# Clustered attention and two dense layers on one core: a list scheduler gets new transfer prices, a later place for sums of squares, and 89 moved priorities

## Chip, core and metric

The kernel runs on one core of one Trainium2 chip. The metric is the device time of one execution in microseconds (us). Before the change the median of three runs is 599.44 us (597.72 to 599.91). PE is the matrix engine, PEld its weight loads, DVE the vector engine, ACT the scalar engine, POOL the third elementwise engine, and SP the engine that issues every DMA of this kernel.

## What is computed

The reference, cut to what matters (2 batches, 8 heads, 768 tokens, 64 elements a head, 16 clusters a head; 1536 tokens of 512 elements in the layers):

```python
q_assign = argmax(q_n @ c_n, -1); k_assign = argmax(k_n @ c_n, -1)   # by head
scores = where(q_assign == k_assign, (q @ k.T) / sqrt(64), -1e9)
attn = softmax(scores) ; x = attn @ v                                # 1536 x 512
h = x @ w_in ; g = h * sigmoid(1.702 * h) ; y = g @ w_out            # 512 -> 2048 -> 512
h = y @ w2_in ; solu = h * softmax(h)                                # 512 -> 1024
out = layernorm(solu) * g_ln @ w2_out                                # 1024 -> 512
```

## The kernel before

**Numbers.** Most products are made of two float16 halves, a high and a low one, in three matmuls each. To cut a weight into halves it is loaded in chunks of 128 x 512 (64-bit on the host, 512 KB a chunk), narrowed by DVE in three steps (`Weight.narrow`, lines 194, 199 and 203), squared and summed by ACT (`Weight.square`, line 216). When all chunks of a group are squared, PE adds the sums over the partitions (`bound`, `power_sum`, line 139, tile `tot`), DVE makes a power of two of them (lines 145 to 153; for `w_out` also lines 1243 to 1251), and then ACT and DVE write the high (line 237) and low (line 240) halves.

**Attention.** The 16 heads of both batches are 16 units u, two to a pair p. A pair's q and k are loaded (`load`), turned and split, their clusters found (`logits`, `cluster_...`), and the operands are put together in the tiles OP1 (64 rows of high halves, 16 of clusters, a row of maxima) and OP2 by DMAs on SP: `place_high` and `place_both` (from the tile `hl`, 64 rows of 6 KB), `place_cluster` (from `oht`, 16 rows), `peak_row` (from `mr`). There are two sets of OP tiles, and pairs take turns at them. A unit has nine steps m. `peak` (PE, line 919) makes scores whose row maxima DVE takes (line 930); `score` (PE, lines 974 and 975) makes them again with the maxima taken off; ACT takes the exponential (line 983) and the float16 high half (`cast`, line 988, sometimes DVE), POOL or DVE the low half (`rest`, line 992), and `value` (PE, lines 1007 to 1011) multiplies with v. The values' own halves are lines 777 and 784 to 790. The result of a pair is split too (`x_high`, line 1037; `x_low`, line 1041, on POOL or DVE) and transposed into `xT` by DMA (line 1047).

**First layer.** 48 blocks `Hidden` of 12 matmuls each (line 1179) follow: three of the four token blocks n, 16 column blocks m. A block is gated by ACT (line 1186), split by ACT (line 1189) and by DVE (line 1197, even m) or POOL (lines 1194 and 1195, odd m). Meanwhile `w_in`'s last three groups and all 16 chunks of `w_out` are converted.

**Order.** All of this, 1825 operations, is put in order by the class `Plan` (line 310), which is run when the program is built. Each operation has a price on each engine that can do it, a list of operations it needs, sometimes a PSUM bank that it takes or frees, and a number `due`. `Plan.order` goes through planned time: of the operations that can start first on an engine it takes the one with the lowest `due`. For SP a price is a pair, the issuing and the transfer, and transfers follow each other in one queue. What the planner finds is written out in that order, engine by engine; on the chip each engine then takes its instructions strictly one after another and waits where one is not ready. Up to 36 us of planned time, PE's planned idle time is filled with matmuls to nowhere (tile `idle`, line 1304).

**After it.** A second plan (line 1329 on, 672 operations) does the rest, from `first_project` (`w_out` on token block 0, lines 1516 to 1527) to the stores. It is the same in both kernels, and its order comes out the same.

The price of a transfer and the sum of squares before the change:

```python
T["PH", p, i] = add(dict(SP=(0.65, 1.94)), n, lambda t, i=i: place_high(p, i), ...)
a = add(
    dict(PE=0.1), NH * NU if after else d + 8, lambda t: bound(t, w.squares(c)), after=sums + (after or []),
    take="acc" if after else "ex", **kw
)
```

Of the kernel before, what the change touches and what calls it, by code (L numbers as in the profile page):

```python
# [21 lines left out]
def kernel(  # L22
# [75 lines left out]
    LN = 512.0  # L98
    WLATE = 4
    WAHEAD2 = 6  # L100
    W0, W1 = 20, 100

    const = ctx.enter_context(tc.tile_pool(name="const", bufs=1))
# [206 lines left out]
    class Plan:  # L310
# [8 lines left out]
        def __init__(self, buffers, limits, loose=False):  # L319
            self.tasks, self.buffers, self.limits, self.loose = [], buffers, limits, loose  # L320

        def add(self, cost, due, emit, after=(), take=None, frees=None, kind=None, shared=False):


            t = dict(
                cost=cost, due=due, emit=emit, after=[a for a in after if a is not None], take=take, frees=frees, kind=kind,
                shared=shared, at=None, id=len(self.tasks), users=[],
            )
            for a in t["after"]:
                a["users"].append(t)  # L330
            t["left"] = len(t["after"])
            self.tasks.append(t)
            return t

        def order(self):
# [11 lines left out]

            def possible(t, eng):
                near = self.loose and eng == "PE"
                at = max([free.get(eng, 0.0)] + [a["end" if near and a["eng"] == eng else "ready"] for a in t["after"]])  # L350
                if eng == "SP":
                    at = max(at, dma - DEPTH)
                if eng == "POOL" or (eng == "DVE" and t["shared"]):
                    at = max(at, port[0])
                if t["take"]:
                    group, limit = self.limits[t["take"]]
                    at = max(at, min(groups[group]))
                    h = sorted(x["until"] for x in held[t["take"]])
                    if len(h) >= limit:
                        at = max(at, h[len(h) - limit])  # L360
                return at
# [174 lines left out]
    def load_first(s):  # L536

        land = space(s).rearrange("p (h j d) -> p h j d", h=2, d=D)
        nc.sync.dma_start(land, (k, q)[s][0, 0:2].rearrange("h (p j) d -> p h j d", p=P))
        return land  # L540
# [120 lines left out]
    def place_high(p, i):  # L661

        move(OP1[p % NS][i][0:D], hl[p][i * D:(i + 1) * D, KH:KH + 2])

    def place_cluster(p, i, s):
        r = (2 * s + i) * C
        move(OP1[p % NS][i][D:D + C, s, :], oht[p][r:r + C, :])
# [9 lines left out]
    def late(x):  # L677

        return [T["PC", 0, 0, 1]] if x else []

    def operands_of(p):
# [3 lines left out]
        land = {}  # L685
        for s in range(2):
            if p == 0:
                a = add(dict(SP=(0.65, 1.09)), n0 - 8, lambda t, s=s: land.update({s: load_first(s)}))
                T["L", p, s, 0] = T["L", p, s, 1] = add(
                    dict(DVE=0.5), n0 - 8, lambda t, s=s: arrange(s, land[s]), after=[a], shared=True  # L690
                )
                continue
            for i in range(2):
                T["L", p, s, i] = add(
                    dict(SP=(0.65, 1.09)), n0 + LDUE if p > 1 else -62, lambda t, s=s, i=i: load(p, s, i),
                    after=[at("TT", p - 1, 2)] + late(True) if p > 1 else [],
                )
        for e in range(3):
# [40 lines left out]
        for i in range(2):  # L739
            u = 2 * (p - NS) + i  # L740
            before = [at("ST", u, NU - 1), at("SM", u, NU - 1)]
            n = n0 + 23 + 4 * i if p else n0 + 10
            T["PH", p, i] = add(
                dict(SP=(0.65, 1.94)), n, lambda t, i=i: place_high(p, i),
                after=[T["TH", p, e] for e in range(3)] + before + late(p),
            )
            for s in range(2 if p or i else 0):
                T["PC", p, i, s] = add(
                    dict(SP=(0.65, 0.14)), n - 15, lambda t, i=i, s=s: place_cluster(p, i, s),
                    after=[b] + before + ([pads[p, i]] if p < NS else []),  # L750
                )
            for e, r in enumerate((0, D)):
                T["PB", p, i, e] = add(
                    dict(SP=(0.65, 1.94)), n + 1 if p else -30 + 12 * i, lambda t, i=i, e=e, r=r: place_both(p, i, r, (QH, QL)[e]),
                    after=[T["TL", p, n] for n in range(3)] + before + late(p or i),
                )

# [39 lines left out]
    def values():  # L797

        sums = []
        for p in range(NH // 2):  # L800
            n = VDA + VDB * p if p else -50
            a = add(dict(SP=(0.47, 1.09)), n, lambda t, p=p: load_values(p), after=late(p >= VFIRST))
            sums.append(add(dict(ACT=0.82), n + 10, lambda t, p=p: values_bound(p), after=[a]))

        def powers(a, n, name):
# [55 lines left out]
    def weights(w, c, due, after=None, then=None, scores=()):  # L861


        sums, parts = [], {}
        kw = dict(tail=2 if after else 0)
        n = CV + bool(scores)
        chunks = range(c * w.group, (c + 1) * w.group)

        def step(i, k):
            if k == 0:  # L870
                parts[i] = w.narrow(i)
            next(parts[i])

        def powers(a):
            w.powers[c] = power_from(a["tile"][:, 0:w.group])
            if then:
                then()

        for i in chunks:
            d = due(i)  # L880
            prev = add(
                dict(SP=(0.47, 1.46)), d, lambda t, i=i: w.load(i),
                after=[narrows[-n] if len(narrows) >= n else None] + list(scores or late(True)), **kw
            )
            for k, x in enumerate((0.34, 0.6, 0.6) if after else (0.4, 1.0, 0.62)):
                prev = add(
                    dict(DVE=x), d + 3 + k, lambda t, i=i, k=k: step(i, k),
                    after=[prev] + (after if after and w is wo else []), shared=True, **kw
                )
            narrows.append(prev)  # L890
            sums.append(add(dict(ACT=0.61), d + 6, lambda t, i=i: w.square(i), after=[prev], **kw))
        a = add(
            dict(PE=0.1), NH * NU if after else d + 8, lambda t: bound(t, w.squares(c)), after=sums + (after or []),
            take="acc" if after else "ex", **kw
        )
        a = add(dict(DVE=0.9), NH * NU if after else d + 8, lambda t, a=a: powers(a), after=[a], frees=a, **kw)
        for i in chunks[0:WLATE if w is wo else w.group]:
            b = add(
                dict(ACT=0.61), d + 12, lambda t, i=i: w.high(i),
                after=[a, at("WL", w, i - 2)], **kw  # L900
            )
            T["WL", w, i] = add(dict(DVE=0.66 if after else 0.9), d + 13, lambda t, i=i: w.low(i), after=[b], shared=True, **kw)
# [383 lines left out]
    for p in range(NH // 2):  # L1286
# [5 lines left out]
        for u in (2 * p, 2 * p + 1):  # L1292
            scores_of(u)
    rest_of_layer()
    order = plan.order()

    idle = ps_b.tile([P, 512], F32, tag="av1", name="idle")
# [718 lines left out]
```

## Time and profile before

| | us |
|---|---|
| median of three runs | 599.44 |
| the profiled execution | 599.53 |
| its span, first to last instruction | 597.8 |
| PE busy in the span | 585.0 |
| DVE, ACT, POOL busy | 460.3, 419.2, 269.2 |
| mean granted TensorE clock | 0.997 |

The profiled execution's time is 1.7 us over its span, which is what lies around the span. The trace shows when each instruction ran, what its engine waited for before it and what ended the wait. A matmul's end is modelled, so PE's busy time hides short waits; what a stretch of PE work costs is read from where the next stretch starts.

### The profile page before, as it was taken

Reading aid. Unit: us, or ns where it says so; the run is one execution under the profiler, and the core shown is the slowest. Engines: PE = TensorE matmul, PEld = TensorE weight load, DVE = VectorE, ACT = ScalarE, POOL = GpSimd, SP = SyncE. Lnnn points to the kernel's source line nnn. Section 1 sums busy time; section 2 is a strip of 40 time slices with the busy share of each in tenths; the row PEclk is TensorE's granted clock in tenths of the full one; section 3 lists DMA queues with packets and bytes.
Section 4 is the critical chain, followed back from the end, with each engine's and each line's share of the span. In section 5 each row is a group of like instructions: output and inputs, shape, how many; then the busy total and the mean of one; then the engine's idle time right before and its main releaser. Section 6 shows DMA issues by size and latency. Waiting matters only on the chain.

```text
span 597.8 us, 12605 instructions
## 1 busy us (share of the span) xinstructions
PE 585.0 (98%) x4784; PEld 386.7 (65%) x4784; DVE 460.3 (77%) x931; ACT 419.2 (70%) x794; POOL 269.2 (45%) x255
## 2 busy tenths in 40 slices
PE   8899999999999999999989999999999999999997
PEld 6687888888888876666645666666655564444444
DVE  6989998799888989888977840884996526997820
ACT  4699989898999988778877446653656623647831
POOL 7269989666787764345653017901200300133100
PEclk9999999999999999999999999999999999999999
DMA  7997979899876127344560440230000430042561
GB/s 189 227 216 163 215 163 184 180 190 185 170 165 119 29 64 203 112 169 135 188 208 1 149 134 2 74 104 0 1 2 0 71 71 0 36 71 72 116 149 53
DMA packets 80884, 68.43 MB, mean 114 GB/s; under 512 B 63748, under 2 KB 66648, under 8 KB 80824
## 3 DMA queue, kind: packets, MB, share of 16 engines
q1 hardware_dynamic: 80824, 67.63, 47.7%
q8 instruction: 37, 0.61, 0.4%
q14 instruction: 23, 0.19, 0.1%
HBM read 34.64 MB, written 3.15 MB: 63 GB/s over the span
## 4 chain that ended last, share of the span: by engine, by line
PE 79%; DVE 11%; DMA 3%; ACT 3%; issue 2%; POOL 1%; SPq 1%; POOLq 0%; DVEq 0%; ACTq 0%
PE bank L1661 20%; PE bank L1482 16%; PE hps L1179 6%; PE bank L1179 5%; PE bank L1516 5%; PE st L974 5%; PE sm L919 5%; PE st L975 4%; PE av L1007 2%; PE av L1011 2%; PE ex L582 2%; PE av L1010 2%; DVE reg L203 2%; DVE reg L199 2%; DVE reg L194 2%
## 5 line engine op out<-in xcount | busy, mean ns | idle before, releaser
L992 POOL TENSOR_TENSOR ph<-p,ph 128x512 f16<-128x512 f32 x108 | 126.9, 1192 | 45.7 <-ACT ph L988 20.4
L1179 PEld LDWEIGHTS <-reg 128*128 128x128 f16 x768 | 75.6, 99 | 49.8 <-issue 1.7
L930 DVE TENSOR_REDUCE nma<-sm 128x1 f32<-128x512 f32 (+1 forms) x144 | 95.9, 680 | 8.8 <-PE sm L919 7.8
L1179 PE MATMUL hps<-xT,reg 128*128 128x384 f16 x576 | 96.2, 330 | 0.0
L1482 PE MATMUL bank<-g,reg 128*128 128x384 f16 x576 | 94.4, 326 | 0.0
L1482 PEld LDWEIGHTS <-reg 128*128 128x128 f16 x576 | 56.4, 98 | 37.2
L1661 PE MATMUL bank<-reg,g 128*128 128x512 f16 (+1 forms) x366 | 75.0, 365 | 0.0
L1194 POOL TENSOR_SCALAR g<-g,scl 128x384 f32<-128x384 f32 x40 | 34.2, 854 | 87.3 <-ACT g L1189 84.3
L1661 PEld LDWEIGHTS <-g 128*128 128x128 f16 x438 | 42.8, 98 | 46.8
L974 PE MATMUL st<-OP 128*128 128x256 f32 (+1 forms) x191 | 70.1, 378 | 2.3 <-DVE nma L930 1.1
L983 ACT ACTIVATE p<-st 128x512 f32<-128x512 f32 x107 | 63.6, 598 | 7.0 <-PE st L975 3.8
L975 PE MATMUL st<-OP 97*128 97x512 f32 (+3 forms) x191 | 62.8, 340 | 0.0
L1007 PE MATMUL av<-vh,ph 128*128 128x65 f16 x576 | 62.2, 194 | 0.0
L1011 PE MATMUL av<-vh,ph 128*128 128x65 f16 x576 | 61.3, 195 | 0.3 <-DVE ph L992 0.2
L1010 PE MATMUL av<-vh,ph 128*128 128x64 f16 x576 | 61.4, 193 | 0.0
L1007 PEld LDWEIGHTS <-ph 128*128 128x128 f16 x576 | 52.8, 99 | 12.5 <-issue 10.3
L919 PE MATMUL sm<-OP 80*128 80x512 f32 x192 | 57.7, 355 | 2.1 <-DMA raw<-in_moe_w_in_dram 0.7
L988 ACT CAST ph<-p 128x512 f16<-128x512 f32 x97 | 58.5, 616 | 1.2 <-PE av L1011 0.6
L1011 PEld LDWEIGHTS <-ph 128*128 128x128 f16 x576 | 53.7, 97 | 0.6 <-DVE ph L992 0.3
L1010 PEld LDWEIGHTS <-ph 128*128 128x128 f16 x576 | 53.8, 97 | 0.1
L1195 POOL TENSOR_TENSOR g<-g,g 128x384 f16<-128x384 f32 x40 | 42.1, 1052 | 3.3
L1864 POOL TENSOR_TENSOR small<-small,mhalf 128x2 f32<-128x2 f32 (+1 forms) x7 | 4.6, 656 | 80.8 <-DVE small L1860 80.8
(252 smaller groups left out, 1168.1 us busy)
## 6 DMA issues: line engine op xcount, KB each, us to landing
OP<-hl SPq DMA_DIRECT2D x48, 384.0 KB, 5.4
raw<-in_moe_w_in_dram SPq DMA_DIRECT2D x24, 512.0 KB, 4.7
raw<-in_moe_w_out_dram SPq DMA_DIRECT2D x24, 512.0 KB, 3.4
xT<-in_v_dram SPq DMA_DIRECT2D x8, 384.0 KB
raw<-in_k_dram SPq DMA_DIRECT2D x12, 192.0 KB, 6.0
raw<-in_q_dram SPq DMA_DIRECT2D x12, 192.0 KB
OP<-oht SPq DMA_DIRECT2D x30, 48.0 KB, 3.7
out_dram<-raw SPq DMA_DIRECT2D x5, 256.0 KB, 2.0
```

The source lines that it names most:

```text
L919: nc.tensor.matmul(t["tile"][:, at], Q1[0:KM, j * P:(j + 1) * P], K1[0:KM, cs], start=True, stop=True)
L930: nc.vector.tensor_reduce(out=out, in_=src, op=ALU.max, axis=AX.X, negate=True)
L974: nc.tensor.matmul(t["tile"][:, at], K2[:, ks], Q2[:, cs], start=True, stop=False)
L975: nc.tensor.matmul(t["tile"][:, at], K1[0:n, ks], Q1[0:n, cs], start=False, stop=True)
L983: nc.scalar.activation(p32s[u, m], t["tile"], AF.Exp, scale=SCALE)
L992: e.tensor_tensor(out=phs[u, m][:, 1], in0=p32s.pop((u, m)), in1=phs[u, m][:, 0], op=ALU.subtract)
L1007: nc.tensor.matmul(av[:, i, :], ph[:, 0, qs], vh[:, u, kt, D:], start=(m == 0 and i == 0), stop=False,)
L1010: nc.tensor.matmul(av[:, i, 0:D], ph[:, 0, qs], vh[:, u, kt, 0:D], start=False, stop=False)
L1011: nc.tensor.matmul(av[:, i, :], ph[:, 1, qs], vh[:, u, kt, D:], start=False, stop=(m == NU - 1 and kt == NJ - 1 and i == NJ - 1),)
L1179: nc.tensor.matmul(self.ps, w1.at(c, m, e), xT[:, x, c, n * TB:(n + 1) * TB], start=(c == 0 and e == x), stop=(c == ND - 1 and e == 1),)
L1482: nc.tensor.matmul(out_, wo.at(f, c, e), lp["g", n][:, x, f, :], start=(f == 0 and e == x), stop=(f == NF - 1 and e == 1),)
L1661: nc.tensor.matmul(out_, data, weight, start=start and i == 0, stop=stop and i == n - 1)
```

## The change

Four things are changed, all in the first plan's input. The instructions are the same but for three of the matmuls to nowhere (57 before, 54 now); only their order and, for 25 operations, the engine differ.

```diff
+    LAG = 3.0
...
-                at = max([free.get(eng, 0.0)] + [a["end" if near and a["eng"] == eng else "ready"] for a in t["after"]])
+                at = max([free.get(eng, 0.0)] + [a["end" if near and a["eng"] == eng else "ready"] + t["lag"] for a in t["after"]])
...
-                a = add(dict(SP=(0.65, 1.09)), n0 - 8, lambda t, s=s: land.update({s: load_first(s)}))
+                a = add(dict(SP=(0.65, 1.0)), n0 - 8, lambda t, s=s: land.update({s: load_first(s)}))
...
-                    dict(SP=(0.65, 1.09)), n0 + LDUE if p > 1 else -62, lambda t, s=s, i=i: load(p, s, i),
+                    dict(SP=(0.65, 1.0)), n0 + LDUE if p > 1 else -62, lambda t, s=s, i=i: load(p, s, i),
...
-                dict(SP=(0.65, 1.94)), n, lambda t, i=i: place_high(p, i),
+                dict(SP=(0.65, 2.05)), n, lambda t, i=i: place_high(p, i),
...
-                    dict(SP=(0.65, 0.14)), n - 15, lambda t, i=i, s=s: place_cluster(p, i, s),
+                    dict(SP=(0.65, 0.5)), n - 15, lambda t, i=i, s=s: place_cluster(p, i, s),
...
-            a = add(dict(SP=(0.47, 1.09)), n, lambda t, p=p: load_values(p), after=late(p >= VFIRST))
+            a = add(dict(SP=(0.47, 1.2)), n, lambda t, p=p: load_values(p), after=late(p >= VFIRST))
...
-                dict(SP=(0.47, 1.46)), d, lambda t, i=i: w.load(i),
+                dict(SP=(0.47, 1.75 if not after else 1.46)), d, lambda t, i=i: w.load(i),
...
-            take="acc" if after else "ex", **kw
+            take="acc" if after else "ex", lag=LAG, **kw
...
+    SHIFTS = {
+        57: 8, 125: -4.5, 145: 1, 163: 4.5, 182: -2, 205: 10, 206: 1.5, 241: -1.5, 250: -2.5, 255: -4, 262: -6,
...
+    }
+    for i, x in SHIFTS.items():
+        plan.tasks[i]["due"] += x
```

`place_both` gets the new price 2.05 as well. `lag` adds 3.0 us of planned time between an operation's inputs and itself; the five sums of squares of `w_in` and `w_out` have it (the later ones belong to the second plan, which has none). `SHIFTS` moves the `due` of 89 of the 1825 operations.

Three places show what comes out. The first is ACT behind the last square of `w_out` (line 216 before, 217 now; `reg_4755` and `reg_4745` are `w_out`'s tile), up to the first high half (line 237, 238). Before:

```order
L216 ACTIVATE junk,wss<-reg_4755 128x512
L1189 ACTIVATE g_4756<-hps,scl 128x384
L1186 ACTIVATE g_5628<-hps,scl 128x384
L216 ACTIVATE junk,wss<-reg_4755 128x512
L1189 ACTIVATE g_4756<-g_5628,scl 128x384
L1186 ACTIVATE hps<-hps,scl 128x384
L1189 ACTIVATE g_4756<-hps,scl 128x384
L1186 ACTIVATE g_5667<-hps,scl 128x384
L1189 ACTIVATE g_4756<-g_5667,scl 128x384
L237 ACTIVATE reg_4755<-reg_4755,scl 128x512 x2
```

Now:

```order
L217 ACTIVATE junk,wss<-reg_4745 128x512 x2
L1190 ACTIVATE g_4746<-g_5617,scl 128x384
L1187 ACTIVATE hps<-hps,scl 128x384
L1187 ACTIVATE g_5641<-hps,scl 128x384
L1190 ACTIVATE g_4746<-hps,scl 128x384
L1190 ACTIVATE g_4746<-g_5641,scl 128x384
L1187 ACTIVATE g_5661<-hps,scl 128x384
L1190 ACTIVATE g_4746<-g_5661,scl 128x384
L1187 ACTIVATE g_5681<-hps,scl 128x384
L1190 ACTIVATE g_4746<-g_5681,scl 128x384
L238 ACTIVATE reg_4745<-reg_4745,scl 128x512 x2
```

The last square is the fourth row before (five operations stand between it and the first high half) and the first row now, where two squares stand together (nine stand between). The same holds on PE: the sum `tot` of `w_out` had 48 matmuls of line 1179, four blocks, behind it and before `first_project`, and has 36 now, three blocks; one block more stands ahead of it. For `w_in`'s groups 1, 2 and 3 the sum stood behind 6, 13 and 22 blocks and stands behind 7, 16 and 23.

The second is SP's queue for pair 4 (units 8 and 9). `OP_0_0` are the tiles of unit 8, `OP_0_1` those of unit 9; 146 and 147 are OP1, 150 and 151 OP2. Before:

```order
L659 DMA OP_0_0_146<-hl 64x2x768
L659 DMA OP_0_0_150<-hl 64x2x768 x2
L659 DMA OP_0_0_146<-oht 16x768 x2
L659 DMA OP_0_1_147<-oht 16x768 x2
L659 DMA OP_0_1_147<-hl 64x2x768
L659 DMA OP_0_1_151<-hl 64x2x768
L659 DMA OP_1_1_149<-mr 1x6x128
L659 DMA OP_0_1_151<-hl 64x2x768
L530 DMA raw<-in_k_dram 128x6x64 x2
L530 DMA raw<-in_q_dram 128x6x64 x2
```

Now:

```order
L660 DMA OP_0_0_146<-hl 64x2x768
L660 DMA OP_0_0_150<-hl 64x2x768 x2
L660 DMA OP_0_0_146<-oht 16x768 x2
L184 DMA raw<-in_moe_w_in_dram 128x1024
L660 DMA OP_0_1_147<-oht 16x768 x2
L660 DMA OP_0_1_151<-hl 64x2x768
L660 DMA OP_1_1_149<-mr 1x6x128
L660 DMA OP_0_1_151<-hl 64x2x768
L531 DMA raw<-in_k_dram 128x6x64 x2
L531 DMA raw<-in_q_dram 128x6x64 x2
L660 DMA OP_0_1_147<-hl 64x2x768
```

A weight chunk has come in between the clusters of unit 8 and those of unit 9, and unit 9's `place_high` (`OP_0_1_147<-hl`) has gone from right behind the clusters to behind two `place_both`, a row of maxima and the four loads of pair 6.

The third is SP's queue for pair 6 (units 12 and 13), in the same tiles, with the transposes of an earlier pair's result (line 1047, now 1048). Before:

```order
L659 DMA OP_0_0_146<-hl 64x2x768
L659 DMA OP_1_0_148<-mr 1x6x128
L659 DMA OP_0_0_150<-hl 64x2x768 x2
L1047 DMA_TRANSPOSE xT<-xh 128x6x128 x2
L659 DMA OP_0_0_146<-oht 16x768 x2
L183 DMA raw<-in_moe_w_in_dram 128x1024
L659 DMA OP_0_1_147<-oht 16x768 x2
L659 DMA OP_0_1_147<-hl 64x2x768
L659 DMA OP_0_1_151<-hl 64x2x768
L659 DMA OP_1_1_149<-mr 1x6x128
L659 DMA OP_0_1_151<-hl 64x2x768
L183 DMA raw<-in_moe_w_in_dram 128x1024
```

Now:

```order
L660 DMA OP_0_0_146<-hl 64x2x768
L660 DMA OP_0_0_150<-hl 64x2x768
L660 DMA OP_1_0_148<-mr 1x6x128
L660 DMA OP_0_0_150<-hl 64x2x768
L1048 DMA_TRANSPOSE xT<-xh 128x6x128
L660 DMA OP_0_0_146<-oht 16x768 x2
L1048 DMA_TRANSPOSE xT<-xh 128x6x128
L660 DMA OP_0_1_147<-oht 16x768 x2
L660 DMA OP_0_1_147<-hl 64x2x768
L660 DMA OP_1_1_149<-mr 1x6x128
L660 DMA OP_0_1_151<-hl 64x2x768 x2
L184 DMA raw<-in_moe_w_in_dram 128x1024 x2
```

Unit 12's clusters (`OP_0_0_146<-oht`) stood behind both transposes and stand between them now; the weight chunk behind them has gone to the end. On DVE and POOL, three of the eight `x_low` (line 1041), those of pairs 2, 5 and 7, have moved from DVE to POOL, and one values' low half, of pair 4, from POOL (lines 784 and 785) to DVE (line 789).

## Rows read from the trace of the kernel before

**Rows 1.** Busy us by stage: length, PE, PEld, DVE, ACT, POOL, clock, DMA share, GB/s.

```profile
18.70:60.00 41.30, 38.48 (x390) 30.68 (x390) 38.97 (x88) 37.59 (x69) 27.51 (x24) 1.00 0.88 201
60.00:222.86 162.86, 160.57 (x2157) 135.97 (x2157) 146.09 (x303) 149.70 (x284) 127.12 (x106) 1.00 0.74 152
222.86:309.46 86.60, 86.60 (x547) 52.37 (x544) 78.83 (x145) 69.55 (x148) 41.63 (x40) 1.00 0.53 164
309.46:311.51 2.05, 0.01 (x2) 0.01 (x1) 1.18 (x3) 1.15 (x4) 0.30 (x1) 1.00 0.66 230
311.51:321.23 9.72, 9.72 (x51) 5.54 (x52) 6.84 (x24) 7.28 (x14) 3.00 (x4) 0.82 0.16 56
```

**Rows 2.** PE's waits, longest first: us in total, times, longest.

```profile
PE tot L139 <- ACT junk L216: 2.0, 1, 2.0
PE st L974 <- DVE nma L930: 1.1, 1, 1.1
PE st L974 <- DVE ph L992: 0.8, 2, 0.6
PE sm L919 <- DMA raw<-in_moe_w_in_dram: 0.7, 1, 0.7
PE sm L919 <- DMA OP<-oht: 0.5, 1, 0.5
```

**Rows 3.** Chain of waits, by time: start, us, what ran.

```profile
311.90 9.49 PE hps L1179 x48
321.39 31.20 PE bank L1516 x192
```

**Rows 4.** PE by time at two of its sums: start, us, instruction.

```profile
234.77 0.28 PE L139 MATMUL tot<-wss,ones 128*128 128x4 f32 x2
...
311.51 0.40 PE L139 MATMUL tot<-wss,ones 128*128 128x16 f32 x2 [2.04 <-ACT junk L216]
```

**Rows 5.** DVE by time, end of the weights' conversion.

```profile
309.97 0.67 DVE L203 SCALAR_TENSOR_TENSOR reg<-raw,reg 128x512 uint32<-128x512 uint32 x1
...
313.58 0.17 DVE L145 TENSOR_REDUCE scl<-tot 128x1 f32<-128x16 f32 x1
...
317.20 1.41 DVE L240 SCALAR_TENSOR_TENSOR reg<-reg,scl 128x512 f16<-128x512 f32 x2 [0.58 <-ACT reg L237]
```

**Rows 6.** ACT by time, the same stretch.

```profile
310.73 0.63 ACT L216 ACTIVATE junk<-reg 128x512 bf16<-128x512 f32 x1 [0.90 <-DVE reg L203]
...
311.36 0.60 ACT L1189 ACTIVATE g<-g,scl 128x384 f16<-128x384 f32 x1
...
313.52 0.61 ACT L1189 ACTIVATE g<-g,scl 128x384 f16<-128x384 f32 x1
316.44 1.33 ACT L237 ACTIVATE reg<-reg,scl 128x512 f16<-128x512 f32 x2 [2.31 <-DVE scl L1251]
```

**Rows 7.** DVE's groups from 222.8 to 311 us: busy, mean ns, idle before.

```profile
L1197 DVE SCALAR_TENSOR_TENSOR g<-hps,scl,g 128x384 f16<-128x384 f32 x21 | 12.5, 607 | 3.8 <-ACT g L1189 3.0 <-POOL g L1194 0.6
...
L1041 DVE TENSOR_TENSOR xh<-xs,xh 128x768 f16<-128x768 f32 x1 | 0.9, 947 | 0.0
```

**Rows 8.** DVE by time, first group of `w_in` that the first layer converts.

```profile
240.29 1.41 DVE L240 SCALAR_TENSOR_TENSOR reg<-reg,scl 128x512 f16<-128x512 f32 x2
```

**Rows 9.** DVE by time, a result's low half in the attention.

```profile
127.24 1.90 DVE L1041 TENSOR_TENSOR xh<-xs,xh 128x768 f16<-128x768 f32 x1
```

**Rows 10.** Groups of the whole execution, nearest prices of moved elementwise work.

```profile
L1041 POOL TENSOR_TENSOR xh<-xs,xh 128x768 f16<-128x768 f32 x5 | 8.3, 1657 | 0.9 <-ACT xh L1037 0.9
...
L1625 DVE SCALAR_TENSOR_TENSOR xT<-y,scl,xT 128x768 f16<-128x768 f32 x5 | 5.0, 1007 | 0.0
```

**Rows 11.** SP by time, loads of pair 6 and a weight chunk.

```profile
113.70 2.24 SPq L530 DMA_DIRECT2D raw<-in_k_dram  x2
...
117.47 1.25 SPq L183 DMA_DIRECT2D raw<-in_moe_w_in_dram  x1
```

**Rows 12.** PE by time, first `peak` of unit 9.

```profile
121.18 0.40 PE L919 MATMUL sm<-OP 80*128 80x512 f32 x1
```

More of the change, by code (lines that the diff above doesn't have):

```diff
@@ L320, in __init__, with add @@
             self.tasks, self.buffers, self.limits, self.loose = [], buffers, limits, loose
-        def add(self, cost, due, emit, after=(), take=None, frees=None, kind=None, shared=False):
+        def add(self, cost, due, emit, after=(), take=None, frees=None, kind=None, shared=False, lag=0.0):
             t = dict(
                 cost=cost, due=due, emit=emit, after=[a for a in after if a is not None], take=take, frees=frees, kind=kind,
-                shared=shared, at=None, id=len(self.tasks), users=[],
+                shared=shared, lag=lag, at=None, id=len(self.tasks), users=[],
             )
@@ L753, in operands_of @@
                 T["PB", p, i, e] = add(
-                    dict(SP=(0.65, 1.94)), n + 1 if p else -30 + 12 * i, lambda t, i=i, e=e, r=r: place_both(p, i, r, (QH, QL)[e]),
+                    dict(SP=(0.65, 2.05)), n + 1 if p else -30 + 12 * i, lambda t, i=i, e=e, r=r: place_both(p, i, r, (QH, QL)[e]),
                     after=[T["TL", p, n] for n in range(3)] + before + late(p or i),
```

8 rows, old and new, of the table SHIFTS are left out of this document.

## Prediction

> **What bounds the kernel now.** I read the busy time by stage first. From 222.86 to 309.46 us PE is busy for the whole stretch, and from 321.23 on the order of both kernels is the same, so what can change lies before 321.23. From 60 to 222.86 PE lacks 2.29 us, from 18.7 to 60 it lacks 2.82, and from 309.46 to 311.51 it stands still; in the stretch after that its mean granted clock is 0.82 [rows 1]. Second I read PE's waits. The longest behind the start is one of 2.0 us: `tot` waits for ACT's last square of `w_out`. The others that have a name are short and lie in the attention: for row maxima (1.1), for a low half of the exponentials (0.8), for a weight chunk ahead in a DMA queue (0.7), for the clusters `oht` (0.5) [rows 2]. Third I read the chain of waits: the first layer's last 48 matmuls take 9.49 us, while `first_project` does 192 matmuls of the same size in 31.20 [rows 3]. At that rate, 0.1625 us each, 48 take 7.80, so the four blocks behind `tot` lost 9.49 - 7.80 = 1.69 us. That is the price of the lower clock: PE came from a gap of 2.04 us [rows 4] and ran part of those blocks at the lower of its two levels, 1.2 instead of 2.4 GHz.
>
> **The last square of w_out.** DVE ends the last narrowing step at 309.97 + 0.67 = 310.64 [rows 5], ACT squares and sums at once, from 310.73, and PE, which reached the sum at 309.47, goes on at 311.51 [rows 4, 6]. Now one block more stands ahead of the sum, 12 x 0.1625 = 1.95 us, so PE reaches it at 311.42 on the old clock. DVE has a little less to do up to there: one `x_low` (0.95) and one block's low half (0.61) have gone from its order, one step of line 203 (0.67) has come in, 0.89 us less [rows 5, 7]. If DVE sets the time, the square is there at 310.6; if the chunk's DMA sets it, at 311.5. The wait is 0 to 0.1 us; I take **-2.04** for it and, since PE then comes to those blocks without a gap, **-1.69** for the clock.
>
> What becomes late next is `first_project`. Behind the sum stand 36 matmuls now, 5.85 us, so PE needs the first low half at about 311.42 + 0.24 + 5.85 = 317.5. ACT has nine operations, not five, between the last square and the first high half. Such operations came every 0.554 us (five from 311.36 to 314.13 [rows 6]), so nine take 5.0 and end at 315.6 to 316.5. DVE's powers took from 313.58 to 316.44 [rows 5, 6], 2.86 us, and cannot start before the sum; they end between 314.5 and 316.4. A high half is half of 1.33 and a low half half of 1.41 [rows 5, 6], so the first low half is there between 317.0 and 317.9. The new wait is 0 to 0.7 us; I take **+0.3**.
>
> The lag also moves the sums of `w_in`. The tight one is group 1: its sum ended at 235.05 and its last low half at 241.70, 6.65 us later [rows 4, 8]. Three blocks stand between the sum and the first matmul on that group, 5.85 us, and the fourth chunk is read by the last three of a block's twelve matmuls, 1.46 later, 7.3 in all. So it costs nothing, covered by those blocks; were the chunk needed at the block's start, it would cost 0.8, which I keep as the bound. Groups 2 and 3 have at least as many blocks as group 1.
>
> **The attention.** At pair 6 a weight chunk stood in SP's queue ahead of what unit 12's `peak` needed, and PE waited 0.7 us [rows 2]. The chunk now stands behind the operands, and unit 12's clusters stand ahead of one transpose: **-0.7** (0 to -0.7). What is late next there is nothing that the trace shows.
>
> The `x_low` of pair 2 stood on DVE ahead of a low half that PE waited for: 1.90 us from 127.24 on [rows 9], inside PE's 0.8 in two waits for `rest` [rows 2]. On POOL it costs 1.66 [rows 10] beside work of PE, but POOL makes low halves too: **-0.6** (0 to -0.8). The other two `x_low` that go to POOL end no wait.
>
> One low half of the values, pair 4, comes to DVE. No row shows line 789 on DVE at this place; the nearest of the same size is line 1625, 1.01 us [rows 10]. From 18.7 to 60 DVE is busy for 38.97 of 41.30 us [rows 1], so what is added there largely shows: **+0.5** (0 to 1.0).
>
> At pair 4 PE waits 0.5 for the clusters [rows 2], and their place behind its other operands in SP's queue is the same. In PE's new order less work stands between the turn of the clusters and that `peak`, which covers the way over DVE and SP, so the wait should grow: **+0.3** (from -0.5, the whole wait, to +0.6, half of one issue of 1.25 [rows 11]).
>
> The rest of the 89 moves and the new transfer prices reorder the same instructions. Nothing is added by them, and dense PE work up to the first products is the same. They can remove what is left of 2.29 + 2.82 us of gaps or add as much again, since DVE is busy for 94% and 90% of these two stretches [rows 1]: **0** (-2.5 to +2.5).
>
> Sum: -2.04 - 1.69 + 0.3 - 0.7 - 0.6 + 0.5 + 0.3 = **-3.9** against the profiled execution's 599.53, which is 0.09 over the median: **595.6 us**.
>
> **The rivals.**
> *The attention gives its share back.* DVE is the chain from 18.7 to 222.86, 146.09 of 162.86 us in its longer part [rows 1], and a wait taken out there may come back one unit later. For it: the waits for DVE's row maxima are the longest of the attention [rows 2]. Against it: three operations leave DVE and one comes. Then -3.4 at the end of the first layer stands alone and the attention adds 1.5: 597.6, no change that can be told. Chance 0.20.
>
> *The clock's loss comes back in another place.* The clock's 1.69 us hung on one gap of 2.04 us; other gaps of PE, 0.5 to 1.1 us [rows 2], had no such loss, and the stretches before 309.46 show a clock of 1.00 [rows 1]. If a gap of that kind arises elsewhere, or the loss is not bound to the gap, the 1.7 stays: 595.6 + 1.7 = 597.3, again no change. The Trainium skill, "TensorE: Matmul & The Clock Gate", section on the HAM clock gate, says that the watch over the engine's activity runs freely and does not start with the kernel. By that rule the same gap costs clock in one execution and none in the next, and the median of before may hold less than 1.69 of it. The three times of before, 597.72, 599.44 and 599.91, lie 1.7 to 2.2 apart, which would fit; one profiled execution cannot show it. Chance 0.13.
>
> *Slower: unit 9's operands come late.* Its `place_high` stands behind a weight chunk, two `place_both`, a row and the four loads of pair 6 now. Before, those loads were issued from 113.70 on and a weight chunk at 117.47 [rows 11]; unit 9's first `peak` ran at 121.18 [rows 12]. All of PE stands behind that `peak`. A wait of 2 us or more would also bring the lower clock, as at 309.46, with its 1.69. To be slower by 3.0 us in spite of the 3.9 gained, the wait must be over 3.9 + 3.0 - 1.69 = 5.2 us, so the operands must land after 126.4 of the old time. The loads end their issue at 117.47, so this needs SP's queue to be some 6 us later than before. It gives 602.6 or more. Chance 0.05.
>
> *More gaps close.* If the moves also take out the waits for maxima and for `oht`, with what stands beside them, some 2.9 us more go: 592.7. Chance 0.07.
>
> That the lag does nothing is ruled out by the order: 36 matmuls stand behind the sum, not 48.
>
> **How the numbers follow.** The forecast has 0.55, and the rivals 0.20, 0.13, 0.05 and 0.07. 0.5% of the median is 3.0 us, about what a measurement of this kernel can tell from no change; faster by more is below 596.4. The forecast's own range is 594.0 to 596.4, and with the closing gaps it gives 0.62 of faster; the first two rivals give 0.33 of no change; the third gives 0.05 of slower. The range goes from 592.7, where more gaps close, to 599.1, where the attention takes all of its bound of 2.5 and the new wait 0.7, with the gains at 161 and 127 us kept at a part of theirs; it leaves out the slower rival and some of the attention's tails.
>
> **What would show it.** Right: no wait of `tot` for `junk` among PE's waits, or one of at most 0.2; a granted clock of 1.00 from the end of that stretch to `first_project`; 36 matmuls at 0.1625 us behind the sum; at most 0.7 us of wait ahead of `first_project`, ended by the powers or the halves of `w_out`. No wait for a weight chunk at pair 6, none of 0.6 for `rest` near pair 2's `x_low`. The second plan takes 276.6 us as before. Wrong: PE before the first products more than 1.5 us later than now, a wait at unit 9's first `peak`, or a clock below 1.00 in any other stretch after the start.

## The result, and the profile after

The changed kernel is slower: a median of 604.94 us (11 runs; 604.10 without one of 2092.52, which the ratio leaves out) beside 600.33 for the kernel before, a ratio of 1.0072 (95% interval 1.0049 to 1.0096). In a second set of 12 runs it took 602.55 beside 600.82, 1.0045 (1.0018 to 1.0071). The forecast was 595.6.

The profiled execution took 602.0, 2.5 us more than that of before. PE's waits in it, with what they waited for, the sum, the count and the longest:

```profile
PE idle L1318 <- DVE idb L113: 2.3, 1, 2.3
PE bank L1530 <- ACT g L1187: 1.1, 1, 1.1
PE sm L920 <- DVE nma L931: 1.0, 2, 0.6
PE ex L553 <- DMA raw<-in_k_dram: 0.9, 1, 0.9
PE st L975 <- DVE nma L931: 0.9, 2, 0.6
PE tx L975 <- DVE OP L948: 0.8, 1, 0.8
PE hps L1180 <- ACT g L1187: 0.6, 1, 0.6
PE bank L1530 <- POOL g L1196: 0.6, 1, 0.6
...
PE bank L1530 <- DVE reg L241: 0.3, 1, 0.3
PE tot L140 <- DVE g L1198: 0.3, 1, 0.3
```

The wait of 2.0 us for the last square, those of 0.7 for a weight chunk and 0.5 for `oht`, and the two for `rest` [rows 2] are gone. In their place stand waits that did not exist: in the first layer (`hps`, `tot`), at `first_project` (`bank`, 2.0 us in three) and for `in_k`. By stage (length, then busy us of PE, PEld, DVE, ACT, POOL, then the clock):

```profile
18.70:60.00 41.30, 38.30 (x385) 30.07 (x383) 36.59 (x82) 36.10 (x67) 24.38 (x21) 0.96 0.88 193
60.00:224.58 164.58, 162.96 (x2169) 138.29 (x2166) 148.26 (x311) 149.88 (x282) 131.18 (x109) 1.00 0.73 150
224.58:315.23 90.65, 89.44 (x564) 53.69 (x560) 79.83 (x146) 69.99 (x152) 44.67 (x39) 1.00 0.56 167
315.23:321.99 6.76, 6.15 (x40) 3.59 (x40) 5.16 (x19) 4.90 (x10) 5.94 (x8) 1.00 0.24 87
321.99:354.75 32.76, 31.37 (x192) 18.60 (x193) 25.84 (x45) 19.53 (x41) 1.50 (x2) 1.00 0.39 127
354.75:600.20 245.45, 242.28 (x1342) 131.11 (x1340) 151.57 (x284) 129.59 (x231) 54.87 (x62) 1.00 0.22 50
```

The stages are cut at the first products of the first layer (224.58, before 222.71), at `tot` (315.23, before 311.51), at `first_project` (321.99, before 321.23) and at its last matmul (354.75). Before, the last of its 192 matmuls started 31.04 after the first; now it starts 32.76 after it. From 354.75 on the program takes what it took. The clock, 1.00 there before [rows 1], is 0.96 in the first row and 1.00 behind `tot`, where it was 0.82. The end of the chain of waits before the last long stretch of PE (start, us, what ran) is no longer the `hps` of [rows 3]:

```profile
313.99 0.72 ACT junk L217 x2
...
316.16 0.48 ACT g L1190
316.66 0.62 DVE g L1198
318.17 0.65 DVE scl L1244
...
319.57 0.81 DVE scl L1245
...
321.16 1.33 ACT reg L238 x2
...
325.17 29.90 PE bank L1530 x183
```

It is read from below: PE's long stretch of `first_project` waits for gates on ACT, these for the high halves of `w_out`, these for the powers on DVE, and these for one low half of a block on DVE (line 1198) that ACT let go at 316.66.

For what follows, **the layer's stretch** is the time from the first products to the last matmul of `first_project`, as PE's rows give it. Before it was 352.27 - 222.71 = 129.56, now 354.75 - 224.58 = 130.17. The forecast said 129.56 - 2.04 - 1.69 + 0.3 = 126.1.

### The profile page after: what moved, and what is told of

It reads as the page before. It is cut to its first block, busy times and chain, and to the rows that moved or that the text cites. A ratio compares the mean times of both kernels' runs of the same rounds, so it can differ in the third digit from the quotient of the medians.

```text
span 600.2 us, 12583 instructions
## 1 busy us (share of the span) xinstructions
PE 586.2 (98%) x4781; PEld 387.1 (64%) x4781; DVE 460.8 (77%) x932; ACT 417.4 (70%) x791; POOL 273.7 (46%) x256
## 4 chain that ended last, share of the span: by engine, by line
PE 74%; DVE 15%; DMA 6%; ACT 3%; issue 1%; SPq 1%; POOL 0%; ACTq 0%; DVEq 0%
PE bank L1675 19%; PE bank L1496 16%; PE st L975 6%; PE bank L1180 5%; PE st L976 5%; PE bank L1530 5%; PE sm L920 5%; DVE reg L204 3%; PE ex L583 3%; PE av L1008 3%; PE av L1012 3%; PE av L1011 2%; DVE reg L200 2%; DMA raw<-in_moe_w_out_dram 2%; DVE g L1198 2%; DVE nma L931 1%
## 5 line engine op out<-in xcount | busy, mean ns | idle before, releaser
L1195 POOL TENSOR_SCALAR g<-g,scl 128x384 f32<-128x384 f32 x40 | 36.3, 908 | 79.7 <-ACT g L1190 79.6
L920 PE MATMUL sm<-OP 80*128 80x512 f32 (+1 forms) x192 | 57.5, 364 | 1.1 <-DVE nma L931 1.0
```

The lines of the kernel that those rows point to most:

```text
L920: nc.tensor.matmul(t["tile"][:, at], Q1[0:KM, j * P:(j + 1) * P], K1[0:KM, cs], start=True, stop=True)
```

## The experiments

Every kernel ran 12 times beside the kernel before. Its mean granted clock is given for every run, so the runs can be sorted by it: of 105 runs of the kernel before 21 had a full clock, with a median of 597.5, and the others 600.5; of 22 of the changed kernel 12, with 602.4, and the others 606.0 (the run of 2092.52 left out). At full clock the change costs 4.9 us.

**The changed kernel again.**

> The changed kernel once more, for a second trace and its spread. Theory: the loss is a row of waits that this order brings in every execution: DVE's row maxima between 45 and 65 us, the turn of pair 3 waiting for in_k at 78 us, gates and sums in the first layer at 264 and 271 us, and the first products of w_out at 322 to 325 us. Then the same rows come back at the same places within 0.3 us each, tot of w_out waits under 0.2 us, and the time is 602 to 606. Rival: the loss is the clock alone, which falls in some executions early in the attention; then executions without a fall are at 599.5 or below, and waits of 321 to 325 us differ from execution to execution.

602.55. The profiled execution had a full clock and ended at 601.09. Its waits are those of the first trace at the same places: 1.1, 0.6 and 0.3 at `first_project`, 0.6 and 0.3 at `hps` and `tot`, 0.9 and 1.0 for row maxima, 1.1 for `in_k`. The layer's stretch is 130.29. So the waits belong to the order. The clock does not explain the loss, since the runs at full clock lose too. Beside the trace of the next kernel, which has a full clock as well (596.50), the 4.6 us between the two are 4.3 in the layer's stretch and 0.3 ahead of it.

**The lag alone.** Kernel before, with

```diff
+    LAG = 3.0
...
-                at = max([free.get(eng, 0.0)] + [a["end" if near and a["eng"] == eng else "ready"] for a in t["after"]])
+                at = max([free.get(eng, 0.0)] + [a["end" if near and a["eng"] == eng else "ready"] + t["lag"] for a in t["after"]])
...
-            take="acc" if after else "ex", **kw
+            take="acc" if after else "ex", lag=LAG, **kw
```

> Kernel before with the lag of 3.0 us alone; the attention's order is that of before, w_out's sum stands behind 46 blocks. Theory (the lag does in the first layer what was forecast, and the attention's new order takes it back): no wait of tot, no fall of the clock behind it, a wait of 0.4 to 1.6 us before or in first_project, 599.5 - 3.7 + 1.0 = about 596.8 (596 to 598.5), and the attention ends where it did. Rival (the first layer itself gives it back, as powers and halves of w_out come too late): the waits from 320 to 326 us are 2.5 us or more and the time is 598.5 to 600.5.

596.68, ratio 0.9938 (0.9915 to 0.9961), the fastest of the study by its median. The layer's stretch is 125.98. PE by time at `tot` and `first_project`, and DVE's first step of the powers:

```profile
313.73 0.29 PE L140 MATMUL tot<-wss,ones 128*128 128x16 f32 x2
313.87 4.06 PE L1180 MATMUL hps<-xT,reg 128*128 128x384 f16 x24
317.77 0.49 PE L1517 MATMUL bank<-g,reg 128*128 128x384 f16 x2
318.51 0.66 PE L1517 MATMUL bank<-g,reg 128*128 128x384 f16 x3 [0.26 <-DVE reg L241]
```

```profile
313.19 0.62 DVE L1198 SCALAR_TENSOR_TENSOR g<-hps,scl,g 128x384 f16<-128x384 f32 x1 [2.03 <-ACT g L1190]
314.06 0.17 DVE L146 TENSOR_REDUCE scl<-tot 128x1 f32<-128x16 f32 x1 [0.26 <-PE tot L140]
```

No wait of `tot`, no fall of the clock there, 24 matmuls behind the sum, and a wait of 0.3 us. DVE has done its low half when the sum is there, and the powers wait for nothing but the sum. In the trace the lag does what was forecast, where nothing else is moved: the layer's stretch is 3.6 shorter than before, and the forecast said 3.4. But the trace of before holds a fall of the clock, and at full clock the lag is worth 1.0 (596.50 against 597.5). Most of the 4 us between the medians goes with the clock: 8 of its 12 runs had a full one, and 2 of the 35 of the kernel before beside them.

**The transfer prices alone.** Kernel before with the changed pairs of numbers at the transfers.

> Kernel before with the new transfer prices alone; the first layer's order is nearly that of before, so tot waits 2 us and the clock falls as before. Theory (the moved priorities bring the attention's loss): within 1.5 us of before, 599 to 602. Rival (the new prices themselves bring the early waits of the attention, 45 to 90 us): 602 or more, with waits at the same places as in the changed kernel.

600.44, ratio 1.0003 (0.9976 to 1.0031): no change. In its trace, at a full clock, `tot` waited 1.20 us and no fall of the clock came behind it. The same place cost 2.04 + 1.69 in the trace of before, so the clock's part is not certain in every execution.

**One sum later.** Kernel before, its order with one operation moved:

```diff
     order = plan.order()
+    i = next(i for i, t in enumerate(order) if t is T["SUM", wo, 0])
+    j = next(j for j in range(i, len(order)) if any(order[j] is T["HP", k] for k in range(48)))
+    order.insert(j, order.pop(i))
```

> Kernel before with one operation moved: w_out's sum stands behind one block more on PE, and everything else keeps its order. Theory: the wait of 2.04 goes to under 0.2 and the 1.69 of the clock with it; DVE's powers and the halves come when they came, the first low half at 317.9, and PE wants it at 317.5, so 0.4 comes back: 599.5 - 3.7 + 0.4 = 596.2 (595.7 to 597.2). Rival (the clock falls in another place or the powers slip by a block): 598 to 600.

599.88, ratio 0.9966 (0.994 to 0.9992), which is in the rival's range; 597.35 in its three runs at full clock. The wait of `tot` and the fall behind it are gone as expected, but 1.5 us came back in `first_project`, not 0.4: 0.70 for a low half on DVE and 0.39 for a gate on ACT are the parts that the trace names. The profiled execution also had the lower clock from 30.3 to 37.1, in a stretch whose order is that of before (length, busy us, and behind them the clock, 0.50):

```profile
30.30:37.10 6.80, 6.36 (x23) 5.32 (x24) 4.60 (x12) 4.98 (x10) 1.16 (x1) 0.50 0.91 205
```

**No moved priorities.** The changed kernel without `SHIFTS`.

> The changed kernel without the 89 moved priorities (lag and new transfer prices stay). Theory: lag and prices do no harm, the moved priorities bring the whole loss. The lag alone ran at 596.7, the prices alone took some 0.8 us of waits out of the attention, w_out's sum stands behind 47 blocks and so leaves less cover before first_project (0.5 to 1 us more of wait): 596.5 (595.5 to 598). Rival (lag and prices together are what loses, as the planner puts the conversions later): 600 or more, with waits from 240 to 285 us.

601.77, ratio 1.0020 (0.9994 to 1.0045), and 599.14 at full clock: a miss. With the new prices beside it the same lag put the sum behind 47 blocks instead of 46, which leaves 12 matmuls of cover. The powers stand behind the low half of block 12, but that held them for only 0.1 us: they began at 317.04, the sum having ended at 316.93, and took 2.86 to the high half. PE by time, the blocks behind the sum and the start of `first_project`:

```profile
316.78 2.11 PE L1180 MATMUL hps<-xT,reg 128*128 128x384 f16 x12
320.72 0.48 PE L1517 MATMUL bank<-g,reg 128*128 128x384 f16 x2 [1.83 <-issue]
```

With 12 matmuls behind the sum PE stood for 1.83 us ahead of `first_project`; no waits came from 240 to 285 us. The layer's stretch is 127.97.

**The attention's moves alone.** The changed kernel with only the moves of operations below number 1453, 68 of the 89 (the expectations count 66 and 23, but the edit parts the 89 into 68 and 21):

```diff
     for i, x in SHIFTS.items():
-        plan.tasks[i]["due"] += x
+        if i < 1453:
+            plan.tasks[i]["due"] += x
```

> The changed kernel with the 66 moved priorities of the attention's operations alone; the 23 of the first layer's are left at their old values. Theory: the waits of 240 to 285 us (some 2.2 us) and of the first products of w_out (2.3 us) go, those of 45 to 90 us stay: 598 (597 to 599.5). Rival (the attention's moves alone make the loss, and the first layer's waits follow from them): 601 or more.

601.35, ratio 1.0023 (0.9999 to 1.0047), which is in the rival's range; 10 of its 12 runs had less than a full clock, and the two others took 599.5 in the mean. The layer's stretch is 127.69: as expected, the waits of 240 to 285 us are gone, and PE is busy through the first layer up to `tot` (first row). In the second row it stands, as in the kernel without any moves, since the sum is behind 47 blocks again:

```profile
232.72:325.14 92.42, 92.42 (x588) 56.20 (x585) 79.10 (x149) 75.10 (x161) 44.17 (x44) 1.00 0.56 170
325.14:328.91 3.77, 2.26 (x17) 1.23 (x15) 3.21 (x20) 2.21 (x5) 1.50 (x2) 1.00 0.00 0
```

Its profiled execution is the slowest of the 12 (607.67), with two falls of the clock in the attention, so it says nothing of the attention's usual end.

**The first layer's 21 moves alone.** The same with `i >= 1453`.

> The changed kernel with the 23 moved priorities of the first layer alone. Theory: they bring waits of PE for gates on ACT and for low halves between 240 and 285 us and at first_project, 2 to 4 us together: 599 (598 to 601). Rival (they cost nothing by themselves, only behind the attention's new order): within 0.7 us of the kernel without any moved priority.

602.48, ratio 1.0053 (1.0029 to 1.0076), above the expected range. PE stood 3.3 us ahead of `first_project`, the clock fell behind that, and the layer's stretch is 130.90. Up to `tot` only 0.5 us was lost, not the changed kernel's 2.1: that part came only with the attention's moves as well.

**The moves of pairs 4 to 7 alone.** Kernel before with the lag and with `774 <= i < 1453`.

> Kernel before with the lag and with the moved priorities of pairs 4 to 7 alone (old transfer prices); up to the operands of pair 4 the order is that of before. Theory: the moves of the attention's second half take 2.5 us of waits out (those at 109, 129, 160 us), and those of its first half bring the waits at 45 to 90 us: 596.7 - 2.5 + 0.3 = 594.5 (593.5 to 596). Rival (a wait taken out comes back one unit later, DVE being the chain): 596 to 597.5.

599.27, ratio 1.0010 (0.9983 to 1.0037): a miss. The waits for clusters and low halves became shorter, but new ones for ACT came, the longest at 153 us (0.92 for an exponential). The first products came at 224.52, 222.8 without the 1.7 of a fall of the clock, which is 0.4 earlier than with the lag alone and not 2.5. The sum went behind 47 blocks, and the layer's stretch is 127.49, 1.5 longer. The rival was right in kind: most of what was taken out of the attention came back.

**The powers first.** The changed kernel with one operation moved:

```diff
     order = plan.order()
+    where = lambda *k: next(i for i, t in enumerate(order) if t is T[k])
+    x = order.pop(where("HL", 40))
+    order.insert(where("POW", wo, 0) + 1, x)
```

> The changed kernel with one operation moved: DVE's low half of block 8 of the third token block stands behind the powers of w_out instead of ahead of them. Theory: in the changed kernel the powers start 1.7 us after the sum, because that low half waits for ACT; now they start with the sum, the first low half of w_out comes some 1.5 us earlier, and the waits ahead of and in first_project fall from 2.4 to about 1 us: 602.6 - 1.4 = 601.2 (600.3 to 602). Rival (gates on ACT and the low half on POOL set these waits, not the powers): within 0.5 us of the changed kernel, 602.1 or more.

601.51; at full clock 599.50, where the changed kernel takes 602.4. The layer's stretch is 128.56, 1.6 to 1.7 less than in the two traces of the changed kernel. DVE's low halves that are left ahead of the powers are done, and the powers' first step waits for the sum alone, as in the kernel with only the lag (DVE by time):

```profile
313.58 0.60 DVE L1200 SCALAR_TENSOR_TENSOR g<-hps,scl,g 128x384 f16<-128x384 f32 x1
315.37 0.17 DVE L146 TENSOR_REDUCE scl<-tot 128x1 f32<-128x16 f32 x1 [1.18 <-PE tot L140]
```

**The sum too late.** The kernel with the lag alone, its sum and powers one block later.

> Kernel before with the lag alone, and w_out's sum and powers one block later still (47 blocks ahead of it, 12 matmuls behind it). Theory: the cover behind the sum decides; the powers, halves and with them first_project come 1.95 us later, and first_project waits about 0.4 + 1.9: 596.7 + 1.7 = 598.4 (597.7 to 599.2). Rival (the place of the sum matters little as long as it does not wait): 596.2 to 597.3.

599.85, ratio 0.9991 (0.9969 to 1.0014), above the expected range. The layer's stretch is 126.98, 1.0 more than with the lag alone, by a wait of 0.79 for a high half ahead of `first_project`; at full clock the runs differ by 0.8 (597.34 against 596.50). The rest of the 3.2 us between the medians is that 9 of its 12 runs had a fall of the clock, against 4 of 12, although the order of the attention is the same in both (clock of 0.997 or less counted as a fall).

**A lag of 1.0.**

> Kernel before with a lag of 1.0 instead of 3.0 us. w_out's sum stands behind 45 blocks and its powers right behind the low half of block 10; one block's low half comes between the powers and the halves. Theory: the last square is there when PE comes to the sum (wait 0 to 0.3), no clock falls there, and first_project waits 0.4 to 1.5 us as in the kernel whose sum alone was moved: 597.5 (596.3 to 598.7). Rival (only the full lag frees the first layer): 599 or more with a wait of tot of 1 us or more.

598.22, ratio 0.9979 (0.9952 to 1.0005). The layer's stretch is 125.55 with no wait at `tot` or `first_project`, the best of all; its sum stands behind 45 blocks, as in the changed kernel. At full clock it takes 596.66, as the lag of 3.0 does, but 8 of its 12 runs had a fall.

**Attention's moves, sum at 46, powers first.** The kernel with the 68 moves, with the sum one block earlier and the powers ahead of the low half of block 12.

> The changed kernel with the attention's 66 moved priorities alone, w_out's sum one block earlier (46 ahead of it) and its powers ahead of the low half of block 12. Theory: the wait of 1.6 us ahead of first_project goes, and what is left over the kernel with the lag alone is the attention's new order: 601.4 - 1.5 = 599.9 (599 to 600.8), with the first products 0.3 to 2 us later than with the lag alone and more falls of the clock early in the attention. Rival (the attention's new order costs nothing): 596.5 to 598.

599.17, ratio 1.0002 (0.9970 to 1.0034), and 597.46 at full clock. The layer's stretch is 126.11, and the first products come at 222.73. With the lag alone they came at 223.26, both at a full clock:

```profile
18.70:60.00 41.30, 38.11 (x391) 29.90 (x392) 38.46 (x83) 36.21 (x67) 25.61 (x22) 1.00 0.84 194
60.00:222.73 162.73, 162.06 (x2157) 137.21 (x2156) 146.72 (x309) 149.74 (x281) 129.96 (x108) 1.00 0.74 151
```

So the attention's new order takes PE's idle time of the longer part from 2.29 [rows 1] to 0.67 and puts some into the shorter one (3.19 instead of 2.82). By the traces it does not cost the 0.3 to 2 us that was expected; by the runs at full clock it costs 1.0 over the lag alone.

Four of these kernels set side by side the layer's stretch under the attention's new order:

| | powers behind a block's low half | powers first |
|---|---|---|
| with the 21 moves | 130.2 (changed kernel), sum behind 45 blocks | 128.6, sum behind 45 |
| without them | 127.7, sum behind 47 | 126.1, sum behind 46 |

The upper row is a clean pair: the place of the powers is worth 1.6. In the lower row it changes nothing, since the powers began 0.04 us behind the sum's end in both kernels; the 1.6 there comes with the sum's place, one block earlier. Each column falls by 2.5 without the 21 moves, but they move the sum as well as the conversions and gates, so the 2.5 belongs to the whole new order of the first layer. Without the moves, with the sum behind 46 blocks, the stretch is the forecast's 126.1.

## Why the prediction was wrong

**The wait of `tot`, -2.04, and the clock behind it, -1.69: right in the trace, the first by luck.** No kernel with the lag waits at `w_out`'s `tot` or has a fall of the clock right behind it. But in the changed kernel the last square was not there at 310.6 to 311.5 of the old time, as the forecast had it. It ended at 314.72, which is 312.85 on the old clock, since the first products came 1.87 later. PE, forecast there at 311.42, came later still, only because it had lost 2.1 us in the first layer (below). PE and ACT of the changed kernel by time:

```profile
315.23 0.29 PE L140 MATMUL tot<-wss,ones 128*128 128x16 f32 x2
```

```profile
314.53 0.19 ACT L217 ACTIVATION_READ_ACCUMULATOR junk<-reg 128x1 f32 x1
```

From the first products to the end of the last square passed 90.1 us, and 45 blocks without a loss take 88.5 (88.53 with the lag of 1.0). In the last kernel of the study, where PE lost nothing, the square was as late, 312.64 - 222.73 = 89.9 (ACT by time):

```profile
312.45 0.19 ACT L217 ACTIVATION_READ_ACCUMULATOR junk<-reg 128x1 f32 x1
```

So with a first layer that lost nothing, `tot` behind 45 blocks would have waited some 1.6 us for the square; that is an estimate, and no run tried it. With the old order of the conversions the square ended 88.5 after the first products in the kernel whose sum alone was moved, and one block more was enough. "DVE has a little less to do up to there" is the premise that did not hold.

The clock's part was taken as certain from one execution. In the prices' trace a wait of 1.20 at this place brought no fall, and the clock also falls at about 30 us in some executions, in orders that are the same there. At full clock the lag alone gave 1.0, not 3.4. In the changed kernel's profiled execution the clock stood at 0.51 from 31.4 to 34.8, behind 3 us in which PE was busy for 2.31, and so gave back what was won behind `tot` (stages as above):

```profile
28.40:31.40 3.00, 2.31 (x12) 1.36 (x12) 3.00 (x8) 3.00 (x8) 0.00 (x0) 1.00 1.21 293
31.40:34.80 3.40, 3.40 (x16) 2.83 (x15) 2.38 (x5) 2.72 (x5) 1.15 (x1) 0.51 1.06 223
```

That is the second rival, and in this execution it held beside the loss. The Trainium skill, "TensorE: Matmul & The Clock Gate", on the HAM clock gate, says that the watch over the engine's activity runs freely. The runs fit: with the order unchanged, 21 of 105 had a full clock and the others did not.

**The wait before `first_project`, +0.3 (0 to 0.7): the first step that failed.** It measured 0.6 ahead of it and 1.7 inside it (32.76 against 31.04), 2.3. The step let the powers end between 314.5 and 316.4: 2.86 us from the sum on, or no later than before. It never asked what stands ahead of them on DVE in the new order, when the inputs of that come, and what POOL does beside them. Two low halves stand ahead, and the second waits for the fourth ACT operation behind the last square, which itself waits for DVE's last narrowing step (ACT by time, and DVE's first step of the powers):

```profile
313.99 0.63 ACT L217 ACTIVATE junk<-reg 128x512 bf16<-128x512 f32 x1 [0.66 <-DVE reg L204]
...
314.62 0.60 ACT L1190 ACTIVATE g<-g,scl 128x384 f16<-128x384 f32 x1
315.13 0.53 ACT L1187 ACTIVATE hps<-hps,scl 128x384 f32<-128x384 f32 x1
315.59 0.57 ACT L1187 ACTIVATE g<-hps,scl 128x384 f32<-128x384 f32 x1
316.05 0.57 ACT L1190 ACTIVATE g<-hps,scl 128x384 f16<-128x384 f32 x1
```

```profile
317.19 0.17 DVE L146 TENSOR_REDUCE scl<-tot 128x1 f32<-128x16 f32 x1
```

The sum ended at 315.52, and the powers began at 317.19, 1.7 later, and took 3.97 to the high half instead of 2.86. Moving that one low half behind the powers took 1.6 us out: shown. But a hold of this kind is not new: before, the powers also began 1.7 behind the sum (311.91 and 313.58), with four blocks as cover. In the kernel with the lag of 1.0, whose sum stands behind 45 blocks too, they began 1.4 behind it and took 2.86, and `first_project` did not wait. What the changed kernel has over that one is 0.2 of hold and 1.1 in the powers themselves, beside POOL's work (last section). That length was not tried by itself.

**"The rest of the 89 moves: 0": the second step that failed.** Its bounds were drawn from PE's gaps in the attention alone. The 21 moves of the first layer were not given a place, since PE had no gap there [rows 1]: a stretch without gaps was taken for one that can't lose. The gates, which free the PSUM banks that PE needs, stand on ACT in one line with squares and high halves. The 45 blocks up to `tot` took 90.65 us; in the last kernel of the study 46 took 313.20 - 222.73 = 90.47, so 45 take 88.52, and 2.1 us were lost. Two of the waits have a name (PE by time):

```profile
265.48 6.01 PE L1180 MATMUL hps<-xT,reg 128*128 128x384 f16 x36 [0.61 <-ACT g L1187]
271.81 0.39 PE L140 MATMUL tot<-wss,ones 128*128 128x4 f32 x2 [0.32 <-DVE g L1198]
```

Ahead of the first of them, ACT by time:

```profile
263.16 0.72 ACT L238 ACTIVATE reg<-reg,scl 128x512 f16<-128x512 f32 x1 [0.54 <-DVE reg L241]
263.79 0.61 ACT L217 ACTIVATE junk<-reg 128x512 bf16<-128x512 f32 x1
...
264.86 0.56 ACT L1187 ACTIVATE g<-hps,scl 128x384 f32<-128x384 f32 x1
```

Here ACT stands 0.54 for a low half on DVE, does a high half and a square, and only then the gate that PE waits for. That the loss comes with the moves is shown: without the 21 (the attention's alone) PE lost nothing up to `tot`, and without the attention's 68 only 0.5. That this queue on ACT is the way is read from the rows and was not tried by itself. The waits with a name make 0.9 of the 2.1; the rest stays open. By the estimate above some 1.6 of the 2.1 stand where `tot` would otherwise have waited. Of the sum of group 1 (0, with 0.8 as the bound) 0.3 came, in the second trace.

**The attention, -0.5: right in its idle time.** The waits at pair 6 and at pair 2's `x_low` are gone, as forecast, and the one at pair 4 went instead of growing. PE's idle time from 18.7 to the first products went from 5.11 [rows 1] to 4.62. New waits for `in_k` and for row maxima make up for part of it. The first products came 1.87 later all the same, which the prediction names as a sign of being wrong, like a clock below 1.00 in another stretch: 1.7 of it is the fall of the clock, and 0.7 is in PE's busy time and stays open. At full clock the two traces of this attention that have one reach them at 223.55 and 222.73, and that of the lag alone at 223.26.

**The rivals.** Unit 9's `peak` had no wait, so the slower rival did not come true; the slowness came from the one stretch that had no rival. The attention did give something back, but it was not what decided.

## What to carry to other kernels

A stretch without gaps is not safe from a new order: where in-order engines free the banks of a full engine, each moved operation there needs its own bound. For an operation that is on the path, look at what stands ahead of it on its engine and when the inputs of that come; a low half held the powers for 1.7 us, and moving it gave 1.6. When several inputs of a list scheduler change together, run each alone: here the lag alone took 3.6 us out of the layer's stretch in its trace and was worth 1.0 at full clock, and with the other two changes the kernel lost 4.9. When a wait is gone, look at whether what it waited for came sooner or the waiting engine came later.

## What the runs showed of the hardware

The powers are operations on 128 x 1 numbers, most of 0.15 us on DVE. Some take up to 0.9, and these end when an operation of POOL ends. Of the changed kernel:

```profile
317.90 0.91 POOL L1196 TENSOR_TENSOR g<-g,g 128x384 f16<-128x384 f32 x1
...
319.46 0.91 POOL L1196 TENSOR_TENSOR g<-g,g 128x384 f16<-128x384 f32 x1
```

```profile
318.09 0.74 DVE L1244 TENSOR_TENSOR scl<-scl 128x1 f32<-128x1 f32 x1
318.75 0.15 DVE L1245 TENSOR_TENSOR scl<-scl 128x1 f32<-128x1 f32 x1
...
319.49 0.89 DVE L1245 TENSOR_TENSOR scl<-scl 128x1 f32<-128x1 f32 x1
```

318.09 + 0.74 is 318.83, and POOL's operation ended at 318.81; 319.49 + 0.89 is 320.38, and POOL's ended at 320.37. Where POOL had nothing to do beside the operations with two inputs (the sum too late), every one of them took 0.15 or 0.16, and the powers took 1.94 to the high half. So the POOL work beside it sets how long such a chain of small operations is: 1.94 there, 2.86 before and 3.97 now. The Trainium skill, "SBUF — State Buffer", on the two sides of SBUF, says that DVE with two inputs from there and GpSimd reading from it take turns at a pair of ports for whole instructions; these rows agree.

The clock fell in some executions and not in others with the order of the attention unchanged, each time to the lower level. Full-clock runs of one kernel lie within about 3 us of each other, and comparing them with full-clock runs of the other shows a change that the mixture hides.
